# Moving QK products, softmax denominators, the exp table load and the output stores in a fused attention and MLP kernel

## The chip, the cores and the metric

The kernel runs as one program on 1 core of a Trainium2 chip. The metric is the device time of one launch in microseconds (us). The core has five engines that work from queues of their own: TensorE (PE: matmuls, with PEld for its weight loads), VectorE (DVE), ScalarE (ACT), GpSimd (POOL) and SyncE (SP, which only issues transfers here). An engine runs its instructions in the order in which they were written, and waits on semaphores where it needs another engine's result.

## The reference

One transformer block on 2048 tokens of width 576, bfloat16 in and out. Layer norm, a QKV projection, attention in which each token sees itself and 7 earlier tokens at distances of 2 (32 heads of 18), an output projection and a residual sum; then a second layer norm (applied twice in a row), an MLP of width 4608 with tanh GELU, and a second residual sum.

```python
idx = pos[:, None] - (jnp.arange(8) * 2)[None, :]
logits = jnp.einsum("bhsd,bhswd->bhsw", q, kg) * scale        # 8 keys of each token
attn = _softmax(jnp.where(mask, logits, -1e9))
o = jnp.einsum("bhsw,bhswd->bhsd", attn, vg)
h = x + o.reshape(B, S, D) @ wo
y = _layernorm(_layernorm(h))
out = h + _gelu(y @ w1 + b1) @ w2 + b2
```

## The kernel before, in words

**Tiles.** Token t lies in tile j = t mod 16, on partition t // 16, so there are 16 tiles of 128 tokens. With that layout the keys at distances of 2 lie in tiles of the same parity, in a ring of 8 (`k_ring`, `v_ring`). `halo` reloads one slot of a ring from a copy in DRAM, shifted by one partition, once the product that read the unshifted slot is done. The 16 tiles are taken in 8 pairs, `GROUPS[0]` to `GROUPS[7]`.

**Stages.** First all QKV products. Then a loop over k = 0 to 7, in which TensorE does the MLP of pair k, while VectorE and ScalarE do the attention of later pairs. The order of each engine is written out by hand (`tc.manual_schedule`): each piece of code that stands in a list is issued at that place. In the loop c, d are the tiles of pair k+1 and e, f those of pair k+2:

- `mlp1` is 4 visits of matmuls of the first MLP product, each followed by GELU on ScalarE. Each visit has 2 or 3 duos of banks. Between the first and the second half of a duo TensorE waits for a no-operation on GpSimd's queue (`marker`), which itself waits for the first half.
- `m1[0]` holds the output sums of the softmax, `pv_sum(c)` and `pv_sum(d)` (`att_pv_a`, line 399, is their first instruction), and the stores and transposing reads that bring the result back as `oT`. `m1[1]` holds the whole QK step of e: `att_qk_a` (line 344, one product of 128 x 4608) and `att_qk_b` (line 353, four halving adds, and line 360). `m1[3]` holds the first sums over GELU outputs (`h_sums`, line 650) that the second MLP product needs.
- `mlp2_fast` does the second MLP product (line 670) with 7 block products in place of 8, in an order given by `steps`. For k = 3 to 5 it is: "wo" (output projection of c and d into the banks pw), "hc" (`ln2_h(c)`, line 463, which reads pw on VectorE, and `ln2_act(c)`, lines 480 to 483), product 1, "b" (a copy of its bank on ScalarE, line 759), "h" (`ln2_h(d)`, `ln2_act(d)`, `put_b2`, more `h_sums`), product 7 into the bank that c's pw held, product 2 into the bank that "b" copied, product 6, "6" (`ln2_send(c)`: lines 489 and 175, and a store), "7" (`ln2_send(d)`; then QK of f; then `att_max`, lines 366 and 367), "d" (a copy, line 759), "rest" (a copy, line 727), "in" (the two transposing reads into `hnT`, line 499, the input of the next pair's `mlp1`; and `reload_x`), product 5, "f" (a copy), "exp" (line 385, and the GELU table again, line 539), product 4, "o1" (line 701: the second tile's output, and an accumulating transfer on GpSimd's queue, `out_sum`, line 772), "4" (`accumulate_h` on GpSimd's queue, line 511, behind the hnT reads; then `att_den`, lines 393 to 395), product 3, "o0".
- For k = 2 the order starts with product 1, and the product of f (line 344) already stands ahead of h, at the end of `m1[3]`.

**The statement that holds a product back.** `ln2_act` leaves the instruction of line 483 (a power on GpSimd, the reciprocal root of LN2) in `root`, and the next `att_qk_a` is made to wait for it:

```python
        if root[0] is not None:
            tc.add_manual_dep(ins, root[0].name, sync_dep, reason="products of QK behind the root of LN2")
```

**Stores.** The two output tiles of the pair before are stored by SP (`out_store`, line 775): tile j1 at "h" (ahead of `put_b2`, line 508), tile j0 at "6". SP also issues the stores of `hn` (lines 193, 194) and the hnT reads, in program order.

Of the kernel before, what the change touches and what calls it, by code (L numbers as in the profile page):

```python
# [8 lines left out]
ACT = mybir.ActivationFunctionType  # L9
ALU = mybir.AluOpType  # L10
# [7 lines left out]
def kernel(  # L18
# [12 lines left out]
    nc = tc.nc  # L31
    P = 128
    _, S, D = A_x.shape
# [3 lines left out]
    W = 8  # L37
# [34 lines left out]
    q_all = wpool.tile([P, NT, D], BF16, name="q_all")  # L72
# [265 lines left out]
            ring = (None, k_ring, v_ring)[t]  # L338
            nc.sync.dma_start(out=ring[j % 2][:, j // 2, :], in_=kv_dram[j, 0:P, t - 1, :])

    root = [None]

    def att_qk_a(j):
        ins = nc.vector.tensor_tensor(out=prod[:], in0=k_ring[j % 2], in1=q_all[:, j, :].unsqueeze(1)  # L344
                                      .to_broadcast([P, W, D]), op=ALU.mult).ins
        if root[0] is not None:
            tc.add_manual_dep(ins, root[0].name, sync_dep, reason="products of QK behind the root of LN2")
            root[0] = None

    def att_qk_add(j, steps):  # L350
        for o, a, c in steps:
# [124 lines left out]
    def ln2_act(j):  # L476
        h = h_of[j]
        y = sb.tile([P, D], BF16, tag="hn", name="hn", bufs=2)
        nmean, var, rstd = (sb.tile([P, 1], F32, tag=f"ln2_{t}", name=f"ln2_{t}", bufs=2) for t in ("nmean", "var", "rstd"))
        nc.scalar.activation(out=y[:], in_=h[:], func=ACT.Identity, scale=-1.0 / D, accum_out=nmean[:])  # L480
        nc.scalar.activation(out=y[:], in_=h[:], func=ACT.Square, bias=nmean[:], accum_out=var[:])
        nc.scalar.activation(out=var[:], in_=var[:], func=ACT.Identity, scale=(1.0 + EPS) / D, bias=eps2[:])  # L482
        ins = nc.gpsimd.tensor_tensor(out=rstd[:], in0=var[:], in1=mhalf[:], op=ALU.pow).ins  # L483
        root[0] = ins if j not in GROUPS[1] else None
        hn[j] = (h, rstd, nmean, y)

    def ln2_send(j):
# [50 lines left out]
    def gelu_table():  # L538
        nc.scalar.activation(out=warm[:], in_=mhalf[:], func=ACT.Gelu_apprx_tanh)


    NM = FT // 2
    fast = GROUPS[2:]
# [138 lines left out]
    def c_(fn, *a):  # L682
        return lambda: fn(*a)
# [4 lines left out]
    def mlp2_fast(g, rows, tags, wo, hooks, first_wo=False):  # L688
        last, summed = wo is None, rows < NM
        q, p, r, s = tags  # L690
        j0, j1 = g
        af = psum_pair(q, "po")
        a, f = (af[:, n, 0:HALF] for n in range(2))
        b, d = psum_pair(p, "po")[:, 0, 0:HALF], None
        o0, o1 = (new_o(j, summed) for j in g)
        flat = kv_ring[1][:].rearrange("p w t d -> p (w t d)")
        rest = halves(flat[:, W * 2 * D - 2 * D:W * 2 * D].bitcast(F32))
        bank = {1: a, 2: a, 3: f, 4: b, 6: b}

        def add(out, x, y):  # L700
            nc.vector.tensor_tensor(out=out, in0=x, in1=y, op=ALU.add)

        def last_out():
            nc.vector.tensor_copy(out=o0[:, HALF:HALF + HALF // 2], in_=f[:, 0:HALF // 2])
            nc.scalar.copy(out=o0[:, HALF + HALF // 2:D], in_=f[:, HALF // 2:HALF])
            nc.sync.dma_start(out=out3[:, j0, HALF:D], in_=o0[:, HALF:D])

        def out0(n0, n1):
            if summed:
                nc.scalar.copy(out=halves(o0), in_=af[:, :, 0:HALF])  # L710
                return
            add(halves(o0)[:, n0:n1], af[:, n0:n1, 0:HALF], halves(x_of(j0))[:, n0:n1])
            nc.sync.dma_start(out=out3[:, j0, n0 * HALF:n1 * HALF], in_=o0[:, n0 * HALF:n1 * HALF])

        def out1():
            if summed:
                add(o1[:, HALF:D], bank[5], o1[:, 0:HALF])
                add(o1[:, 0:HALF], b, o1[:, 0:HALF])
                out_sum(j1)
                return  # L720
            add(o1[:, 0:HALF], b, rest[:, 0])
            add(o1[:, HALF:D], bank[5], rest[:, 1])
            nc.sync.dma_start(out=out3[:, j1, :], in_=o1)

        def do_rest():
            if summed:
                nc.scalar.copy(out=o1[:, 0:HALF], in_=bank[7])
                return
            add(rest, bank[7].unsqueeze(1).to_broadcast([P, 2, HALF]), halves(x_of(j1)))

        def take():
            bank[7], bank[5] = (psum_pair(tag, "po")[:, 0, 0:HALF] for tag in (r, s))

        lo, hi, all_ = (0, SR), (SR, rows), (0, rows)
        seed = {"b": (1, 6), "d": (6, 5), "f": (5, 3)}
        does = {
            "wo": lambda: wo((r, s)), "e": take, "rest": do_rest, "o1": out1,
            "o0": lambda: last_out() if last else out0(0, 2), "lo": lambda: out0(0, 1),
            "11": lambda: plain(0, 0, a, rows), "12": lambda: plain(0, 1, f, rows),
            "21": lambda: plain(1, 0, b, rows), "22": lambda: plain(1, 1, bank[5], rows),  # L740
        }
        if rows < NM:
            steps = [(1, all_), "b", "wo", "hc", "h", "e", (2, all_), "11", (6, all_), "d", "6", "7", (7, all_), "rest"] if not first_wo \
                else ["wo", "hc", (1, all_), "b", "h", "e", (7, lo), (2, all_), (6, all_), "6", "d", "rest", "7", "11"] if rows == SR \
                else ["wo", "hc", (1, all_), "b", "h", "e", (7, lo), (2, all_), (6, all_), "6", "7", "d", "11", (7, hi), "rest"]
            steps += ["in", (5, all_), "f", "exp", (4, all_), "21", "22", "o1", "4", (3, all_), "12", "o0", "3"]
        elif not last:
            steps = ["wo", "hc", (1, all_), "b", "h", "e", (7, lo), (6, all_), "6", "d", "7", (2, all_), (7, hi), "rest", "in",
                     (5, all_), "f", (4, all_), "o1", "4", (3, all_), "o0"]
        else:  # L750
            steps = ["e", (1, lo), (7, lo), (1, hi), "b", "h", (7, hi), "rest", (6, all_), "d", (2, all_), "lo",
                     (5, all_), "f", (4, all_), "o1", (3, all_), "o0"]
        for step in steps:
            if isinstance(step, tuple):
                product(step[0], bank[step[0]], *step[1])
            elif step == "f" and last:
                add(f, bank[5], x_of(j0)[:, HALF:D])
            elif step in seed:
                nc.scalar.copy(out=bank[seed[step][1]], in_=bank[seed[step][0]])
            else:  # L760
                call([does[step]] if step in does else hooks.get(step, ()))
# [22 lines left out]
    with tc.manual_schedule(engines={ENG.PE, ENG.Activation, ENG.DVE, ENG.SP, ENG.Pool}):  # L784
# [227 lines left out]
        for k, g in enumerate(GROUPS):  # L1012
# [38 lines left out]
            if k < 6:  # L1051
                m1[1] = m1.get(1, []) + [c_(att_qk_one, e, 0)]
                m1.setdefault(3, [])
                if k == 2:
                    m1[0] += [c_(pv_sum, d), c_(send_o, d), c_(read_o, d)]
                    m1[3] += [c_(w2_sums, 0, 8, (2, 3)), c_(w2_sums, 8, 12, (2, 3)), c_(w2_sums, 12, 14, (0, 1)), c_(w2_sums, 14, 16, (0, 1)),
                              c_(att_qk_a, f), c_(halo, f, 1)]
                early = {2: (), 5: (0,)}.get(k, (0, 2))
                if k == 3:
                    m1[3] += [c_(w2_sums, 12, 14, (2, 3)), c_(w2_sums, 14, 16, (2, 3))]  # L1060
                m1[3] += [c_(h_sums, 0, min(rows, SR), early)]
                if k == 5:
                    x["h"] += [c_(h_sums, 0, SR, (2,)), c_(h_sums, 0, SR, (1, 3))]
                else:
                    x["h"] += [c_(h_sums, 0, SR, [t for t in range(4) if t not in early])]
                if rows > SR:
                    x["h"] += [c_(h_sums, SR, rows)]
                x["7"] += [c_(att_qk_one, f, 1) if k > 2 else c_(att_qk_b, f, 1), c_(att_max, (e, f))]
                x["exp"] += [c_(exps, e, f)]
                x["4"] += [c_(att_den, e, f)]  # L1070
            else:
                if k == 6:
                    ring1_free[0] = True
                    m1[1].append(c_(w2_sums, 16, NM))
                m1[3] = m1.get(3, []) + [c_(h_sums, 0, SR)]
                if k == 7:
                    mid[3] = {1: [c_(h_sums, SR, 16)]}
                    x["h"] += [c_(h_sums, 16, NM)]
# [16 lines left out]
                wo = lambda tags: wo_visit((c, tags[0]), (d, tags[1]))  # L1095
            if 3 <= k < 7:
                x["hc"].insert(0, c_(out_sum, GROUPS[k - 1][0]))
                x["h"].insert(0, c_(out_store, GROUPS[k - 1][1]))
                x["6"].insert(0, c_(out_store, GROUPS[k - 1][0]))
            mlp1(g, mlp1_plan(p, q, r, s, (r, s, p)), m1, mid)  # L1100
            if 3 <= k < 7:
                mlp2_fast(g, rows, (s, p, q, r), wo, x, True)
# [34 lines left out]
```

## Time and profile before

| | |
|---|---|
| median of 3 runs | 364.18 us (364.08 to 366.05) |
| the profiled execution: its time, its span | 363.63 us, 361.8 us |
| PE, DVE, ACT, POOL busy | 98%, 82%, 65%, 13% of the span |
| granted TensorE clock | 1.00 |
| start of the MLP of pairs 3, 4, 5, 6, 7 on PE | 180.85, 217.35, 253.14, 289.25, 324.92 us |
| VectorE's first output sum in pairs 3, 4, 5, 6 (line 399) | 181.30, 218.30, 254.41, 290.21 us |
| VectorE's first h in pairs 2, 3, 4, 5 (line 463) | 165.65, 201.35, 237.51, 273.08 us |

Lines of a timeline are: start, duration, engine, line, operation, output <- input, shapes, number of instructions, and in brackets the idle time before it with what ended it. Times are us from the span's start. A row of an engine ending in q is the queue that issues transfers.

### The profile page before, as it was taken

Reading aid. Unit: us, or ns where it says so; the run is one execution under the profiler, and the core shown is the slowest. Engines: PE = TensorE matmul, PEld = TensorE weight load, DVE = VectorE, ACT = ScalarE, POOL = GpSimd, SP = SyncE. Lnnn points to the kernel's source line nnn. Section 1 sums busy time; section 2 is a strip of 40 time slices with the busy share of each in tenths; the row PEclk is TensorE's granted clock in tenths of the full one; section 3 lists DMA queues with packets and bytes.
Section 4 is the critical chain, followed back from the end, with each engine's and each line's share of the span. In section 5 each row is a group of like instructions: output and inputs, shape, how many; then the busy total and the mean of one; then the engine's idle time right before and its main releaser. Section 6 shows DMA issues by size and latency. Waiting matters only on the chain.

```text
span 361.8 us, 11435 instructions
## 1 busy us (share of the span) xinstructions
PE 356.3 (98%) x4883; PEld 291.2 (80%) x4883; DVE 296.3 (82%) x417; ACT 235.5 (65%) x519; POOL 46.4 (13%) x61
## 2 busy tenths in 40 slices
PE   8999999999999999999999999999999999999996
PEld 5678777888778877887788778877887788779974
DVE  4999999999989999997799898989899998520431
ACT  4779846798646783668566955695669566706620
POOL 2241004000112020201110202020102110201000
PEclk9999999999999999999999999999999999999999
DMA  7986999973447884731454555445544252253001
GB/s 235 324 257 175 261 197 294 346 266 72 135 89 109 225 172 71 135 72 51 107 86 103 71 121 85 90 83 123 86 74 113 61 85 72 47 110 53 2 3 34
DMA packets 62980, 46.07 MB, mean 127 GB/s; under 512 B 32192, under 2 KB 60736, under 8 KB 62928
## 3 DMA queue, kind: packets, MB, share of 16 engines
q1 hardware_dynamic: 59024, 41.42, 44.2%
q0 software_dynamic: 3744, 3.84, 9.9%
q8 instruction: 38, 0.62, 0.7%
q10 hardware_dynamic: 160, 0.07, 0.1%
q14 instruction: 14, 0.11, 0.1%
HBM read 23.16 MB, written 12.42 MB: 98 GB/s over the span
## 4 chain that ended last, share of the span: by engine, by line
PE 91%; DMA 5%; ACT 1%; DVE 1%; issue 0%; ACTq 0%; SPq 0%
PE pm L217 37%; PE po L670 25%; PE pq L217 13%; PE po L582 10%; PE pw L217 5%; DMA oT<-td 2%; DMA xnT<-xd 1%; ACT h_all L563 1%; DMA wqh_sb<-in_A_wqkv_dram 1%; DMA x_all<-in_A_x_dram 1%; PE xt_pt L182 1%; DVE kv_ring L650 0%; DVE ln_stats L149 0%; PE h_pt L182 0%; PE o_pt L182 0%
## 5 line engine op out<-in xcount | busy, mean ns | idle before, releaser
L217 PE MATMUL pm<-hnT,w_sb 64*128 64x256 bf16 x2304 | 143.0, 269 | 0.1
L563 ACT ACTIVATE h_all<-pm,b_sb 128x256 f16<-128x256 f32 (+1 forms) x288 | 108.6, 496 | 51.2 <-PE pm L217 50.5
L217 PEld LDWEIGHTS <-w_sb 64*128 64x128 bf16 x2304 | 113.5, 94 | 13.4 <-issue 1.8
L670 PEld LDWEIGHTS <-h_all 128*128 128x128 f16 x480 | 46.2, 98 | 13.6 <-issue 1.6
L217 PE MATMUL pq<-wq_sb,xnT 64*128 64x288 bf16 x768 | 54.5, 283 | 0.3 <-DMA wq_sb<-in_A_wqkv_dram 0.2
L217 PEld LDWEIGHTS <-xnT 64*128 64x128 bf16 x864 | 41.8, 94 | 11.2 <-DMA xnT<-xd 0.4
L353 DVE TENSOR_TENSOR prod<-prod 128x2304 bf16<-128x2304 bf16 (+1 forms) x64 | 44.2, 691 | 2.0
L399 DVE TENSOR_TENSOR prod<-kv_ring,probs 128x4608 bf16<-128x4608 bf16 x16 | 40.9, 2558 | 2.6 <-DMA kv_ring<-kv_dram 2.2
L344 DVE TENSOR_TENSOR prod<-kv_ring,q_all 128x4608 bf16<-128x4608 bf16 x16 | 40.8, 2551 | 2.5 <-POOL ln_rstd L483 2.0
L217 PE MATMUL pm<-hnT,w1h_sb 64*128 64x256 bf16 x288 | 39.5, 269 | 0.0
L670 PE MATMUL po<-w2a_sb,h_all 128*128 128x288 bf16 (+1 forms) x262 | 35.8, 286 | 0.0
L405 DVE TENSOR_TENSOR prod<-prod 128x2304 bf16<-128x2304 bf16 (+1 forms) x32 | 33.9, 1058 | 1.1
L582 PEld LDWEIGHTS <-h_all 128*128 128x128 bf16 x288 | 27.9, 98 | 7.9 <-issue 1.0
L670 PEld LDWEIGHTS <-kv_ring 128*128 128x128 f16 x252 | 24.6, 98 | 6.3
L582 PE MATMUL po<-w2a_sb,h_all 128*128 128x288 bf16 x224 | 28.5, 286 | 0.0
L772 POOL DMA_DIRECT2D x_all<-o_sb x12 | 10.7, 889 | 126.9 <-PE pw L217 55.6
L650 DVE TENSOR_TENSOR kv_ring<-h_all 128x1536 f16<-128x1536 f16 (+3 forms) x9 | 6.8, 760 | 16.4 <-ACT h_all L563 16.4
L217 PE MATMUL pw<-wo_sb,oT 64*128 64x288 bf16 x256 | 19.6, 283 | 0.7 <-DMA oT<-td 0.7
L670 PE MATMUL po<-w2b_sb,h_all 128*128 128x288 bf16 (+1 forms) x122 | 19.7, 286 | 0.1
L162 POOL TENSOR_TENSOR ln_rstd<-ln_veps,mhalf 128x1 f32<-128x1 f32 (+2 forms) x14 | 13.4, 965 | 48.4 <-DVE ln_veps L156 33.3
L483 POOL TENSOR_TENSOR ln_rstd<-ln_var,mhalf 128x1 f32<-128x1 f32 x13 | 9.2, 708 | 80.9 <-ACT ln_var L482 80.9
L217 PEld LDWEIGHTS <-oT 64*128 64x128 bf16 x288 | 13.5, 94 | 5.3 <-DMA oT<-td 1.3
(115 smaller groups left out, 404.2 us busy)
## 6 DMA issues: line engine op xcount, KB each, us to landing
w_sb<-in_B_w_dram SPq DMA_DIRECT2D x6, 768.0 KB, 5.8
kv_ring<-kv_dram SPq DMA_DIRECT2D x28, 144.0 KB, 2.9
w2a_sb<-in_B_w_dram SPq DMA_DIRECT2D x4, 1008.0 KB, 7.1
kv_dram<-kv_ring SPq DMA_DIRECT2D x13, 288.0 KB, 3.3
td<-q_all SPq DMA_DIRECT2D x14, 144.0 KB, 1.8
x_all<-in_B_b_dram SPq DMA_DIRECT2D x14, 144.0 KB, 3.8
td<-hn SPq DMA_DIRECT2D x14, 144.0 KB, 1.8
x_all<-h POOLq DMA_DIRECT2D x14, 144.0 KB, 4.7
```

Source lines behind the costliest of these rows:

```text
L162: nc.gpsimd.tensor_tensor(out=rstd[:], in0=veps[:], in1=mhalf[:].to_broadcast([P, n]), op=ALU.pow)
L217: last = nc.tensor.matmul(duo["g"][r ^ swap][i], lhsT=lhsT, rhs=rhs, start=(swap == 0 and i == 0 and kt == 0), stop=(swap == 1 and kt == K ...
L344: ins = nc.vector.tensor_tensor(out=prod[:], in0=k_ring[j % 2], in1=q_all[:, j, :].unsqueeze(1) .to_broadcast([P, W, D]), op=ALU.mult).ins
L353: nc.vector.tensor_tensor(out=prod[:, :, o * H:o * H + n], in0=prod[:, :, a * H:a * H + n], in1=prod[:, :, c * H:c * H + n], op=ALU.add)
L399: nc.vector.tensor_tensor(out=prod[:].rearrange("p w (d h) -> p w d h", h=H), in0=v_ring[j % 2].rearrange("p w (d h) -> p w d h", h=H), in ...
L405: nc.vector.tensor_tensor(out=prod[:, 0:n, :], in0=prod[:, 0:n, :], in1=prod[:, n:2 * n, :], op=ALU.add)
L483: ins = nc.gpsimd.tensor_tensor(out=rstd[:], in0=var[:], in1=mhalf[:], op=ALU.pow).ins
L563: pace[0] = nc.scalar.activation(out=hT(grp)[:, f, 0:N], in_=ps[:, r, i * N:(i + 1) * N], func=ACT.Gelu_apprx_tanh, bias=b1_sb[:, f:f + 1] ...
L582: nc.tensor.matmul(banks[half], lhsT=hT(grp)[:, f, i * P:(i + 1) * P], rhs=w2_rows(f)[:, half * HALF:(half + 1) * HALF], start=(f == 0), s ...
L650: nc.vector.tensor_tensor(out=s_slot(t, m0, m1), in0=a, in1=b, op=alu)
L670: nc.tensor.matmul(bank, lhsT=l, rhs=r, start=start, stop=stop, skip_group_check=True)
L772: nc.gpsimd.dma_start(out=x_of(j), in_=o_of.pop(j), accum_op=ALU.add)
```

## The change

For pairs k = 3 to 5 the product of f (with the `halo` behind it) moves from "7" to the end of `m1[3]`, ahead of h, and its wait for the root of LN2 is gone. For k = 2, where the product already stood there, the first two of the four adds go with it. `att_den` moves from "4" to right behind `exps`, so that on VectorE its three instructions stand ahead of the two of line 701. The exp table, loaded until now by the exp itself behind the copy "f", is loaded by a one-column exp (`exp_table`) ahead of "in", that is, behind the copy "rest" and ahead of the copy "f"; the exp then needs no load. The two `out_store` of k = 3 to 6 stand together ahead of the sends at "6". On TensorE the order of instructions stays as it is; on GpSimd too.

```diff
     def att_qk_a(j):
-        ins = nc.vector.tensor_tensor(out=prod[:], in0=k_ring[j % 2], in1=q_all[:, j, :].unsqueeze(1)
-                                      .to_broadcast([P, W, D]), op=ALU.mult).ins
-        if root[0] is not None:
-            tc.add_manual_dep(ins, root[0].name, sync_dep, reason="products of QK behind the root of LN2")
-            root[0] = None
+        nc.vector.tensor_tensor(out=prod[:], in0=k_ring[j % 2], in1=q_all[:, j, :].unsqueeze(1)
+                                .to_broadcast([P, W, D]), op=ALU.mult)
...
+    def exp_table():
+        nc.scalar.activation(out=warm[:], in_=mhalf[:], func=ACT.Exp)
...
-            steps += ["in", (5, all_), "f", "exp", (4, all_), "21", "22", "o1", "4", (3, all_), "12", "o0", "3"]
+            steps += ["table", "in", (5, all_), "f", "exp", (4, all_), "21", "22", "o1", "4", (3, all_), "12", "o0", "3"]
...
-                              c_(att_qk_a, f), c_(halo, f, 1)]
+                              c_(att_qk_a, f), c_(halo, f, 1), c_(att_qk_add, f, ((0, 0, 9), (0, 0, 4)))]
...
                 m1[3] += [c_(h_sums, 0, min(rows, SR), early)]
+                if k > 2:
+                    m1[3] += [c_(att_qk_a, f), c_(halo, f, 1)]
...
-                x["7"] += [c_(att_qk_one, f, 1) if k > 2 else c_(att_qk_b, f, 1), c_(att_max, (e, f))]
-                x["exp"] += [c_(exps, e, f)]
-                x["4"] += [c_(att_den, e, f)]
+                x["7"] += [c_(att_qk_b, f, 1, 0 if k > 2 else 2), c_(att_max, (e, f))]
+                x["table"] = [exp_table]
+                x["exp"] += [c_(exps, e, f), c_(att_den, e, f)]
...
-                x["h"].insert(0, c_(out_store, GROUPS[k - 1][1]))
-                x["6"].insert(0, c_(out_store, GROUPS[k - 1][0]))
+                x["6"][0:0] = [c_(out_store, j) for j in GROUPS[k - 1][::-1]]
```

More of the change, by code (lines that the diff above doesn't have):

```diff
@@ L339, in halo @@
             nc.sync.dma_start(out=ring[j % 2][:, j // 2, :], in_=kv_dram[j, 0:P, t - 1, :])
-    root = [None]
     def att_qk_a(j):
-        ins = nc.vector.tensor_tensor(out=prod[:], in0=k_ring[j % 2], in1=q_all[:, j, :].unsqueeze(1)
-                                      .to_broadcast([P, W, D]), op=ALU.mult).ins
-        if root[0] is not None:
-            tc.add_manual_dep(ins, root[0].name, sync_dep, reason="products of QK behind the root of LN2")
-            root[0] = None
+        nc.vector.tensor_tensor(out=prod[:], in0=k_ring[j % 2], in1=q_all[:, j, :].unsqueeze(1)
+                                .to_broadcast([P, W, D]), op=ALU.mult)
     def att_qk_add(j, steps):
@@ L482, in ln2_act @@
         nc.scalar.activation(out=var[:], in_=var[:], func=ACT.Identity, scale=(1.0 + EPS) / D, bias=eps2[:])
-        ins = nc.gpsimd.tensor_tensor(out=rstd[:], in0=var[:], in1=mhalf[:], op=ALU.pow).ins
-        root[0] = ins if j not in GROUPS[1] else None
+        nc.gpsimd.tensor_tensor(out=rstd[:], in0=var[:], in1=mhalf[:], op=ALU.pow)
         hn[j] = (h, rstd, nmean, y)
```

## The prediction

> **What bounds the kernel now.** I read the page's busy shares and chain first.
>
> ```profile
> PE 356.3 (98%) x4883; PEld 291.2 (80%) x4883; DVE 296.3 (82%) x417; ACT 235.5 (65%) x519; POOL 46.4 (13%) x61
> PE 91%; DMA 5%; ACT 1%; DVE 1%; issue 0%; ACTq 0%; SPq 0%
> ```
>
> TensorE is busy for 98% and no matmul is removed, so the change can win no more than the waits of TensorE that it touches. The list of waits has them (the third row is a wait of VectorE):
>
> ```profile
> PE pw L217 <- DMA oT<-td: 0.7, 2, 0.6
> PEld L217 <- DMA oT<-td: 1.3, 2, 0.9
> DVE prod L344 <- POOL ln_rstd L483: 2.0, 2, 1.0
> ```
>
> Two waits for oT: in pair 3 the output projection took 3.03 us (198.54 to 201.57) where pair 4 took 2.30 (235.05 to 237.35), 0.73 lost; in pair 5 0.15. The most to be won is 0.9 us, 0.25%. A measurement of this kernel can tell about 0.5%, 1.8 us, from no change.
>
> So the question is what the moved work makes late. VectorE's timeline around h of pair 4:
>
> ```profile
> 236.63 0.96 DVE L650 TENSOR_TENSOR h_all<-h_all 128x1536 f16<-128x1536 f16 x1
> 237.51 1.42 DVE L463 TENSOR_TENSOR h<-pw,x_all 128x576 f32<-128x576 f32 x2
> 243.25 2.56 DVE L344 TENSOR_TENSOR prod<-kv_ring,q_all 128x4608 bf16<-128x4608 bf16 x1 [1.00 <-POOL ln_rstd L483]
> 250.56 0.69 DVE L367 TENSOR_TENSOR logits<-logits,peak 128x512 f32<-128x512 f32 x1
> 251.17 0.94 DVE L701 TENSOR_TENSOR o_sb<-po,o_sb 128x288 f32<-128x288 f32 x2
> 252.03 1.03 DVE L393 TENSOR_REDUCE den<-logits 128x64 f32<-128x512 f32 x1
> 254.41 2.56 DVE L399 TENSOR_TENSOR prod<-kv_ring,probs 128x4608 bf16<-128x4608 bf16 x1
> ```
>
> Before h there is no idle time: h is late because VectorE is. What hangs on h is in the ScalarE and TensorE timelines:
>
> ```profile
> 240.20 0.39 ACT L759 COPY po<-po 128x288 f32<-128x288 f32 x1
> 239.32 3.35 PE L670 MATMUL po<-w2a_sb,h_all 128*128 128x288 f16 x26
> ```
>
> The copy "b" ends 3.08 us after h begins, because ScalarE does c's statistics first. The 26 matmuls are 12 of product 7 and 14 of product 2; at 0.1225 us each product 2 begins at 240.79, and it writes the bank that "b" reads: only 0.2 us to spare.
>
> **The change, part by part.** All times below start at h, on the trace's clock.
>
> *Pair 2.* VectorE idles 2.47 us before h (163.18 to 165.65, for TensorE's pw). The two adds moved there cost 1.36 + 0.69, with gaps 2.1, and fit. Behind h 2.1 us go, so the maximum ends at 173.7 in place of 175.83. Then ScalarE is late: "rest" ends at 173.53, table and warm-up take 1.28 + 0.20, "f" 0.38, so the exp runs 175.45 to 176.1. Denominators 2.35 (252.03 to 254.38 in pair 4), line 701 0.95: output sums begin at 179.45 in place of 181.30.
>
> *Pair 3.* The sums feed oT, so oT comes 1.85 us earlier: TensorE's 0.73 is won. But on VectorE line 399 to h took 20.05 us (181.30 to 201.35) and now holds the product as well, 2.6: h at 202.1, 0.75 late. Product 2 would begin at 203.54 + 1.47 - 0.73 = 204.28; the copy it waits for ends at 202.1 + 3.08. With 0.06 for the semaphore that is 0.96 of stall. Net +0.23, and 0.15 from the next item.
>
> *The wait for the root that is taken away.* The product no longer idles 1.0 us, but the big add of line 353 (1.36 us) now runs when GpSimd wants to begin d's root, 5.16 us after h (242.67). GpSimd's timeline shows what that costs, with VectorE's of pair 1:
>
> ```profile
> 131.47 1.53 POOL L483 TENSOR_TENSOR ln_rstd<-ln_var,mhalf 128x1 f32<-128x1 f32 x1 [1.33 <-ACT ln_var L482]
> 240.45 0.75 POOL L483 TENSOR_TENSOR ln_rstd<-ln_var,mhalf 128x1 f32<-128x1 f32 x1 [2.47 <-ACT ln_var L482]
> 242.67 0.55 POOL L483 TENSOR_TENSOR ln_rstd<-ln_var,mhalf 128x1 f32<-128x1 f32 x1 [1.47 <-ACT ln_var L482]
> 131.24 1.35 DVE L640 TENSOR_TENSOR x_all<-w2a_sb 128x2304 f16<-128x2304 bf16 x1
> ```
>
> A root took 0.55 beside an idle VectorE; 131.47 + 1.53 = 133.00 is 0.41 after the end of the VectorE instruction that was running (132.59). The add will run 4.78 to 6.14 after h, so d's root ends at 6.56, not 5.71; d's send and the copy "d" come 0.5 later, 8.1 after h, where product 5 wants it at 8.0: 0.1 of stall, plus 0.05 for hnT, in pairs 3 and 4 (in pair 5 one more sum lies there). Bounds: 0 and 0.5 each. The Trainium skill's page "SBUF — State Buffer", section "Who interferes with whom", says that a VectorE instruction with two SBUF inputs and a GpSimd one that reads SBUF exclude each other, whichever starts first; it speaks against taking this wait away, and by it the root waits the add's remainder, 0.98 us; if it did not hold, 0.3 us of the whole sum would go.
>
> *Behind h.* Line 399 began 16.90 us after h. Minus the product 2.6, minus the root 1.0: 13.3. But the exp, which line 701 hid, lies open now: product 2 starts 3.14 after h; products 2, 6 and 5 take 1.96 each and two short blocks 0.98, so product 5 ends 10.1 after h with the 0.1 above; "f" takes 0.4, exp 0.65, denominators 2.35, line 701 0.95: 14.5. So VectorE's loop is 19.2 + 2.6 + 14.5 = 36.3 us against TensorE's 35.79: VectorE sets the pace, which the change does not shorten. The table is covered: "f" is needed by the blocks behind product 4, over 2 us later. Were it not, up to 1.3 us per pair. The Trainium skill's page "ScalarE: Activation LUTs", section "What ACT_TABLE_LOAD costs", adds a drain of 1.38 us to each load; no row shows it (after the load at 215.69 the warm-up begins 1.30 later), and by it the output sums would come 1.4 later and pairs 4 and 5 lose about 1.4 each, an estimate.
>
> *Pair 4.* Output sums at 202.1 + 14.5 = 216.6, h 21.8 later at 238.4. Product 2 is due at 240.79 + 0.38 = 241.17 and free at 241.54: +0.4, with the root +0.5. Shift now 0.9.
>
> *Pair 5.* Sums at 252.9. Line 399 to h took 18.67, less 0.32 idle, plus 2.6: h at 273.85. The product also needs the `halo` of e, issued 270.19 - 1.5 with 2.9 to land: 0.3 more, h at 274.15. Product 7 needs the sum that ended 2.29 after h: 276.5. It was due at 275.43 - 0.15 + 0.9 = 276.2. Shift 0.9 - 0.15 + 0.35 = 1.1; bounds of the halo 0 and 1.
>
> *Pair 6.* Only SP's order changes: one more `out_store` goes ahead of d's store.
>
> ```profile
> 316.05 0.43 SPq L193 DMA_DIRECT2D td<-hn  x1
> 320.53 2.53 SPq L499 DMA_TRANSPOSE hnT<-td  x2
> ```
>
> This store landed 4.3 us after issue, behind three transfers, where c's (313.75, nothing ahead) took 1.8: 0.8 for each transfer ahead. The second transpose (issued 321.8, 2.9 to land) arrives at 324.7 to 324.8; TensorE ended at 324.85 and began at 324.92. Nothing is spare, so 0.43 (one issue) to 0.8 reaches TensorE; I take 0.6. In pairs 3 to 5 I cost SP's new order at 0: the `halo` of f waits for the product, which ends as h begins, and `put_b2` behind it waits for h anyway; the second store waits for line 772's transfer (237.12 + 3.3 = 240.4), and the next thing behind it, c's store of hn, is ready only 6.1 after h, at 244.5. Each us by which that transfer lands past this would be paid in full.
>
> Sum: 0.4 + 0.5 + 0.2 + 0.6 = 1.7, rounded to 1.8 for the gaps left out. Span 363.6; the profiled execution took 1.83 more than its span: 365.4. It lay 0.55 below the median: **366.0 us**.
>
> **Rivals.**
>
> *A. Nothing is late.* If ScalarE's copies slip in, or VectorE's gaps shrink by the 0.5 us that its loop is over TensorE's, only the oT waits go: 0.9 less, 363.3. For it: the root's 1.0 is real. Against it: the copy had 0.2 to spare. It decides if pair 4's h begins before 238.0.
>
> *B. The accumulating transfers make GpSimd's queue late.* Line 701 now stands behind the denominators; behind it on GpSimd's queue come line 772 (begins 0.3 later), the two of line 511 (2.1 us in all), and then the marker on which TensorE waits 2.19 us into the next pair. Pair 4: line 701 ends at 252.9, so 252.9 + 0.3 + 0.6 + 2.1 = 255.9, and TensorE needs it at 253.14 + 0.9 + 2.19 = 256.2. Beyond 0.3 us of extra issue time each us is paid at pairs 3, 4 and 5: with 1 us, +2.1, 368.1. For it: line 511 will begin inside line 399's product. Against it: 1.75 us for both in pair 1 (147.39), beside line 405's adds.
>
> *C. The table costs nothing and does nothing.* The built order has one load for each, so a second load is not a rival of weight.
>
> **How the numbers follow.** Main case 0.56, 365.2 to 367.2, a little over half of it above the line of 0.5% (366.0): 0.31 slower, 0.25 same. B, or several narrow covers (GpSimd 0.3, hnT of pair 3 0.1) failing: 0.24, all slower. A 0.19: 0.15 same, 0.04 faster. Else 0.01 slower. Range 363.1 (A) to 368.6 (B and the upper bounds): 0.04 faster, 0.40 same, 0.56 slower.
>
> **What would show it.** Right: no oT wait of TensorE in pairs 3 and 5; first h at about 202.1, 238.4 and 274.2; a wait of TensorE for "b" or h ahead of product 2 or 7 of 0.3 to 1 us in each of these pairs; d's root longer than 1 us in pairs 3 and 4; VectorE idle about 0.7 us or more for the exp; pair 7's MLP behind a wait for hnT. Wrong: TensorE at 98% with MLP starts as before (A), or waits of TensorE's weight loads at the first marker of a pair (B).

## The result and the profile after

| | before | after |
|---|---|---|
| median of 19 runs each, same chip | 364.18 us (362.65 to 366.05) | 366.32 us (364.82 to 369.45) |
| ratio, 95% interval | | 1.0064 [1.0041, 1.0087] |
| the profiled execution: its time, its span | 363.63 us, 361.8 us | 367.51 us, 365.7 us |
| step of pairs 3, 4, 5, 6 | 36.50, 35.79, 36.11, 35.67 us | 37.82, 36.21, 36.49, 36.16 us |

A step is the time from the start of a pair's MLP on TensorE to that of the next pair. The change made the kernel 2.1 us slower, 0.6%. In the profiled executions the four steps cost 1.32, 0.42, 0.38 and 0.49, together 2.61. The other 1.28 us between the spans lies before the MLP of pair 0, which the change does not touch: TensorE waited 1.2 us for `q_all` there, 0.2 before. That start varied from 68.05 to 72.82 us over all kernels told of here, so kernels are compared below by their steps.

The page of the changed kernel, busy shares and chain:

```profile
PE 356.9 (98%) x4883; PEld 291.8 (80%) x4883; DVE 295.6 (81%) x417; ACT 236.0 (65%) x523; POOL 47.8 (13%) x61
PE 70%; DVE 13%; DMA 8%; ACT 5%; issue 2%; SPq 1%; POOL 0%; ACTq 0%; DVEq 0%; POOLq 0%
```

The busy row does not show the loss: 98% as before. The chain does: TensorE's share of it fell from 91% to 70% and VectorE's rose from 1% to 13%. The list of TensorE's waits (total, how often, longest) shows where:

```profile
PE po L667 <- DVE h L458: 1.0, 1, 1.0
PE pm L217 <- DMA hnT<-td: 0.9, 2, 0.6
PE po L667 <- ACT po L756: 0.7, 1, 0.7
PE po L667 <- DVE h_all L647: 0.5, 1, 0.5
```

The waits for oT are gone; h, the copy of its bank, the sums of `h_all` and hnT have taken their place. (The numbers of these lines are 2 to 6 lower in the changed kernel: 342 was 344, 458 was 463, 493 was 499.) TensorE's timeline in pair 3, where half of the loss is:

```profile
202.13 1.89 PE L667 MATMUL po<-w2a_sb,h_all 128*128 128x288 bf16 x14
203.85 0.41 PE L667 MATMUL po<-w2b_sb,h_all 128*128 128x288 bf16 x2
205.27 1.63 PE L667 MATMUL po<-w2a_sb,h_all 128*128 128x288 f16 x12 [1.01 <-DVE h L458]
207.60 1.88 PE L667 MATMUL po<-w2a_sb,h_all 128*128 128x288 bf16 x14 [0.70 <-ACT po L756]
```

The first two rows are product 1, the third product 7, the fourth product 2. Product 7 was due at 203.85 + 0.25 = 204.10 and began at 205.27, when h had read its bank; product 2 was due 1.47 later, at 206.74, and began at 207.60, behind the copy "b". 1.17 + 0.86 lost, less the 0.73 that oT cost before: 1.30 of the 1.32. VectorE's timeline of the same pair tells why h was late:

```profile
180.32 2.55 DVE L394 TENSOR_TENSOR prod<-kv_ring,probs 128x4608 bf16<-128x4608 bf16 x1
...
187.42 2.56 DVE L394 TENSOR_TENSOR prod<-kv_ring,probs 128x4608 bf16<-128x4608 bf16 x1 [1.88 <-DMA kv_ring<-kv_dram]
...
202.00 2.55 DVE L342 TENSOR_TENSOR prod<-kv_ring,q_all 128x4608 bf16<-128x4608 bf16 x1
204.47 1.41 DVE L458 TENSOR_TENSOR h<-pw,x_all 128x576 f32<-128x576 f32 x2
```

The output sums came early, as meant, but the second product of them waited 1.88 us for the reload of the v ring (0.18 before). In pair 4, the pair shown of before, VectorE ran like this:

```profile
237.80 2.55 DVE L342 TENSOR_TENSOR prod<-kv_ring,q_all 128x4608 bf16<-128x4608 bf16 x1
240.27 1.42 DVE L458 TENSOR_TENSOR h<-pw,x_all 128x576 f32<-128x576 f32 x2
...
251.42 1.06 DVE L388 TENSOR_REDUCE den<-logits 128x64 f32<-128x512 f32 x1 [1.10 <-ACT logits L380]
...
253.71 0.94 DVE L698 TENSOR_TENSOR o_sb<-po,o_sb 128x288 f32<-128x288 f32 x2
254.57 2.55 DVE L394 TENSOR_TENSOR prod<-kv_ring,probs 128x4608 bf16<-128x4608 bf16 x1
```

The product stands ahead of h; the sums begin 14.30 us after h where they began 16.90 after it; and VectorE now idles 1.10 us for the exp. d's root on GpSimd in pair 3, and SP's issues in pair 6:

```profile
209.63 1.26 POOL L478 TENSOR_TENSOR ln_rstd<-ln_var,mhalf 128x1 f32<-128x1 f32 x1 [1.47 <-ACT ln_var L477]
```

```profile
319.04 0.85 SPq L772 DMA_DIRECT2D out_dram<-x_all  x2
319.94 0.46 SPq L193 DMA_DIRECT2D td<-hn  x1
320.44 0.44 SPq L194 DMA_DIRECT2D td<-hn  x1
324.21 2.54 SPq L493 DMA_TRANSPOSE hnT<-td  x2
```

d's root took 1.26 in place of 0.55. In pair 6 the transposing read was issued 31.56 us after the pair's MLP began, before 31.28 (320.53 - 289.25).

### The profile page after: what moved, and what is told of

It is laid out like the page before. It is cut to its first block, busy times and chain, and to the rows that moved or that the text cites. A ratio compares the mean times of both kernels' runs of the same rounds, so it can differ in the third digit from the quotient of the medians.

```text
span 365.7 us, 11430 instructions
## 1 busy us (share of the span) xinstructions
PE 356.9 (98%) x4883; PEld 291.8 (80%) x4883; DVE 295.6 (81%) x417; ACT 236.0 (65%) x523; POOL 47.8 (13%) x61
## 4 chain that ended last, share of the span: by engine, by line
PE 70%; DVE 13%; DMA 8%; ACT 5%; issue 2%; SPq 1%; POOL 0%; ACTq 0%; DVEq 0%; POOLq 0%
PE pm L217 28%; PE po L667 15%; PE pq L217 13%; PE po L579 10%; PE pw L217 3%; DVE prod L394 3%; ACT h_all L560 2%; DVE prod L342 2%; DMA kv_ring<-kv_dram 2%; DVE prod L400 2%; DVE prod L348 2%; DMA x_all<-in_A_x_dram 1%; DMA xnT<-xd 1%; DMA wqh_sb<-in_A_wqkv_dram 1%; DMA td<-hn 1%
## 5 line engine op out<-in xcount | busy, mean ns | idle before, releaser
L478 POOL TENSOR_TENSOR ln_rstd<-ln_var,mhalf 128x1 f32<-128x1 f32 x13 | 10.6, 816 | 84.3 <-ACT ln_var L477 84.3
```

## The experiments

The theory to test: the product of f ahead of h costs about 5 us by itself, because VectorE's loop then grows past TensorE's 35.8; the denominators ahead of line 701 and the early table give most of that back; the missing wait for the root costs little because the product no longer stands next to it; the stores cost some tenths in pair 6. Rivals: the new place of the denominators costs (through GpSimd's queue), or the early output sums do (through the reload of the v ring). Rows with the same median of before ran on one chip and share its runs; the steps are those of one execution.

| kernel | median, before beside it | ratio, 95% | steps of pairs 3, 4, 5, 6 |
|---|---|---|---|
| x1_product | 369.65, 364.65 | 1.0154 [1.0130, 1.0178] | 38.34, 37.97, 38.36, 35.54 |
| x2_stores | 364.62, 364.65 | 1.0009 [0.9985, 1.0034] | 35.90, 36.28, 36.20, 36.05 |
| x3_product_back | 368.19, 364.65 | 1.0101 [1.0063, 1.0138] | 35.78, 37.97, 37.76, 36.84 |
| x5_no_root_wait | 366.49, 364.65 | 1.0052 [1.0031, 1.0073] | 37.10, 37.06, 35.79, 35.59 |
| x4_pair2 | 363.75, 363.86 | 0.9997 [0.9977, 1.0017] | 35.78, 35.78, 36.36, 35.71 |
| x6_stores_back | 366.91, 363.86 | 1.0069 [1.0047, 1.0091] | 38.07, 36.10, 35.79, 35.93 |
| x7_den_back | 370.59, 363.86 | 1.0167 [1.0136, 1.0199] | 38.31, 38.83, 36.73, 35.87 |
| x8_no_table | 370.19, 363.86 | 1.0172 [1.0128, 1.0217] | 37.92, 38.68, 37.18, 36.26 |
| x9_no_accumulate | 366.41, 363.48 | 1.0084 [1.0057, 1.0110] | 37.08, 35.88, 37.02, 36.80 |
| x10_again | 365.55, 363.48 | 1.0067 [1.0045, 1.0088] | 37.55, 35.88, 35.93, 35.91 |

**x1_product: the kernel before, with the product of f moved ahead of h alone** (and, as in the change, without its wait for the root).

```diff
+                if k > 2:
+                    m1[3] += [c_(att_qk_a, f), c_(halo, f, 1)]
...
-                x["7"] += [c_(att_qk_one, f, 1) if k > 2 else c_(att_qk_b, f, 1), c_(att_max, (e, f))]
+                x["7"] += [c_(att_qk_b, f, 1), c_(att_max, (e, f))]
```

> Before, with one part of the change alone: for pairs 3 to 5 the product of f stands ahead of h and waits for no root. The step of a pair is the start of the next pair's MLP on TensorE minus its own; before: 36.50, 35.79, 36.11, 35.67 us for pairs 3 to 6; changed kernel: 37.82, 36.21, 36.49, 36.16. Theory (h on VectorE is the limit, and the product ahead of it is what costs): worse than the whole change, since nothing else makes VectorE's loop shorter: first h of pair 3 at 203.9, products 7 and 2 wait some 2 us together there, and the loop 21.8 + about 16.2 = 38 us against 35.8, so steps of 38.5, 37.9 and about 38, +5 to +6 us in all. Rival (the product is free, the other parts cost): steps within 0.4 us of before, at most +1 us.

Measured: 5.0 us slower. VectorE's timeline of its pair 4 shows that the time the product freed behind h was not used:

```profile
241.36 1.41 DVE L460 TENSOR_TENSOR h<-pw,x_all 128x576 f32<-128x576 f32 x2
...
254.55 0.95 DVE L698 TENSOR_TENSOR o_sb<-po,o_sb 128x288 f32<-128x288 f32 x2 [3.14 <-PE po L667]
...
257.81 2.56 DVE L396 TENSOR_TENSOR prod<-kv_ring,probs 128x4608 bf16<-128x4608 bf16 x1
```

The output sums begin 16.45 us after h, hardly earlier than with the product behind it (16.90), because the o1 add waits 3.14 us for TensorE and the denominators stand behind it. The product is paid in full ahead of h and gives nothing back. The theory held.

**x7_den_back: the changed kernel with the denominators behind the o1 add.**

```diff
-                x["exp"] += [c_(exps, e, f), c_(att_den, e, f)]
+                x["exp"] += [c_(exps, e, f)]
+                x["4"] += [c_(att_den, e, f)]
```

> The changed kernel with the denominators put back behind the o1 add (line 698 of the changed kernel); exp and its early table stay. Theory (VectorE's loop sets the pace; the product ahead of h alone makes it 38.4, and the denominators ahead of the o1 add give back 2 of that): output sums begin 2 to 2.6 us later after h (16.5 to 16.9 in place of 14.3), steps of pairs 4 and 5 about 38 in place of 36.2 and 36.5, step of pair 3 unchanged or some tenths shorter (37.3 to 37.8), since the later output sums no longer meet the accumulating transfers; time 3 to 4 more, 369.5. Rival (the denominators wait for the exp anyway, 1.1 us, so their place is worth little): output sums 1 us later, steps 36.5 to 37, time 1 more.

```profile
217.39 0.95 DVE L698 TENSOR_TENSOR o_sb<-po,o_sb 128x288 f32<-128x288 f32 x2 [3.55 <-PE po L667]
218.25 1.03 DVE L388 TENSOR_REDUCE den<-logits 128x64 f32<-128x512 f32 x1
...
220.63 2.56 DVE L394 TENSOR_TENSOR prod<-kv_ring,probs 128x4608 bf16<-128x4608 bf16 x1
```

Measured: 6.7 us slower than before, 4 to 5 more than the changed kernel. The sums begin 16.79 us after the h at 203.84, and pair 4's step is 38.83. The wait of 3.55 for TensorE is the room that the denominators fill in the changed kernel: their move is a gain there, 2.5 us in pair 3 and 2.1 in pair 4 on VectorE. Pair 5's step was 36.73, not 38; pair 4 had given TensorE 3 us of delay already, which is the likely reason. Pair 3's step was not shorter (38.31). Its sums came late enough that VectorE did not wait for the v ring at all, and from the sums (181.49) to h (203.84) it took 22.35 us, the figure without that wait; but the sums began 2.3 us later than in x10_again (179.16), so oT was late again and cost 0.62. In pair 3 the loss thus has two forms of one size: late sums, or early sums that wait for the reload.

**x8_no_table: the changed kernel without the early table load.**

```diff
-                x["table"] = [exp_table]
```

> The changed kernel without its separate load of the exp table: the exp loads its table itself, behind the last bank copy. Theory (the table is on VectorE's path, because the denominators wait for the exp): exp 1.3 us later, VectorE's wait for it 2.2 to 2.4 in place of 1.1, output sums 15.6 us after h in place of 14.3, steps of pairs 4 and 5 37.0 to 37.5 in place of 36.2 and 36.5, time about 2 more, 368. Rival 1 (the exp has slack): steps and time as in the changed kernel. Rival 2 (a load costs a drain of 1.38 beside its 1.28, as the Trainium skill's page 'ScalarE: Activation LUTs', section 'What ACT_TABLE_LOAD costs', says): exp 2.7 later, steps 38 to 38.5; that sentence alone rests on the page.

```profile
220.73 1.04 DVE L388 TENSOR_REDUCE den<-logits 128x64 f32<-128x512 f32 x1 [2.55 <-ACT logits L380]
...
223.86 2.55 DVE L394 TENSOR_TENSOR prod<-kv_ring,probs 128x4608 bf16<-128x4608 bf16 x1
...
230.83 2.56 DVE L394 TENSOR_TENSOR prod<-kv_ring,probs 128x4608 bf16<-128x4608 bf16 x1 [1.68 <-DMA kv_ring<-kv_dram]
```

The wait for the exp grew in pair 3 from 1.15 and 1.18 (two executions of the changed kernel) to 2.55, and the sums begin 15.68 us after h (208.18), within 0.1 of the theory. The time is 6.3 us over before, 4 over the changed kernel, where 2 were expected. (The steps are those of its slowest execution, 374.46; 2.6 us of that are a wait of TensorE for xnT ahead of the pairs.) Pair 4's step rose by more than expected, to 38.68, because the later sums, with 1.68 for the v ring among them, made oT late too: TensorE waited 1.28 for it at 243.41. So the early load is worth its place: the table stood on VectorE's path. The growth of the wait, 1.37 to 1.40, is the 1.28 of the load and 0.1. The Trainium skill's page "ScalarE: Activation LUTs", section "What ACT_TABLE_LOAD costs", adds a drain of about 1.38 us to each switch; no run here shows one, since 2.66 would have made the wait 3.8, and the exp began 1.30 after its load (220.07 against 218.77).

**x5_no_root_wait: the kernel before with the wait for the root taken off, the product left behind h.**

```diff
-        if root[0] is not None:
-            tc.add_manual_dep(ins, root[0].name, sync_dep, reason="products of QK behind the root of LN2")
```

> Before, with nothing changed but that the product of f no longer waits for the root of LN2 (it stays behind h). Theory (VectorE's product and GpSimd's root keep each other off): the product begins 4.8 us after h, the root of d wants to begin at 5.16 and ends 0.42 after the product, at about 7.8 in place of 5.7: a root of 2.6 us in pairs 3 and 4, d's send and the copy d 2 us late, TensorE waits 1 to 1.6 us ahead of product 5 in those pairs, total +1 to +3 us. Rival (they share nothing): the root stays at 0.55 to 0.75 us, VectorE is 1.0 us earlier in pairs 3 and 4, and the time is the same or up to 0.3 us less.

GpSimd's, VectorE's and TensorE's timelines:

```profile
207.08 2.45 POOL L480 TENSOR_TENSOR ln_rstd<-ln_var,mhalf 128x1 f32<-128x1 f32 x1 [1.47 <-ACT ln_var L479]
```

```profile
206.57 2.55 DVE L344 TENSOR_TENSOR prod<-kv_ring,q_all 128x4608 bf16<-128x4608 bf16 x1
```

```profile
211.10 1.63 PE L667 MATMUL po<-x_all,kv_ring 128*128 128x288 f16 x12 [0.31 <-ACT po L756]
247.76 1.63 PE L667 MATMUL po<-x_all,kv_ring 128*128 128x288 f16 x12 [0.72 <-ACT po L756]
```

The product ended at 209.12, the root at 209.53, 0.41 later: a 2.45 us root in place of 0.55, and TensorE waits for the copy behind it, 0.31 and 0.72 where 1 to 1.6 were expected. The time rose by 1.8 us, so the wait that the change removes was worth its 1.0 us of idle VectorE while the product stood there. In the changed kernel only a 1.35 us add stands there, and the root's 1.26 made no product wait: from product 6 to product 5 TensorE took 2.94 us in pairs 3 and 4 (209.56 to 212.50, 245.36 to 248.30), as before (206.97 to 209.91).

**x3_product_back: the changed kernel with the product behind h again.**

```diff
-                if k > 2:
-                    m1[3] += [c_(att_qk_a, f), c_(halo, f, 1)]
...
-                x["7"] += [c_(att_qk_b, f, 1, 0 if k > 2 else 2), c_(att_max, (e, f))]
+                x["7"] += [c_(att_qk_one, f, 1) if k > 2 else c_(att_qk_b, f, 1, 2), c_(att_max, (e, f))]
```

(with the wait for the root)

> The changed kernel with the product of pairs 3 to 5 put back behind h and behind the root; all else as changed. Theory (product ahead of h is the cost): no wait of TensorE for h or for the copy b in pairs 3 to 5; the oT waits of pairs 3 and 5 stay away or shrink; steps about 35.9, 35.8, 35.9 and 36.2 for pair 6 (stores): 0.3 to 0.5 us below before, within noise of it, and 2 us or more below the changed kernel. Rival (denominators ahead of line 701, or the table, or the stores cost it): steps of pairs 3 to 5 stay above 36.2.

TensorE's rows, and the o1 add on VectorE:

```profile
219.88 2.36 PE L217 MATMUL pm<-hnT,w_sb 64*128 64x256 bf16 x40 [0.45 <-POOLq L227]
...
237.56 0.66 PE L217 MATMUL pw<-wo_sb,oT 64*128 64x288 bf16 x8 [1.39 <-DMA oT<-td]
217.67 0.94 DVE L704 TENSOR_TENSOR o_sb<-po,o_sb 128x288 f32<-128x288 f32 x2
```

The theory failed for pairs 4 to 6. Pair 3's step of 35.78 shows its wait for oT gone. But the first MLPs of pairs 4, 5 and 6 wait for the marker behind GpSimd's queue (0.45; the weight loads beside them 0.72), oT is 1.39 and 0.99 late in pairs 4 and 5, and VectorE waits 2.10 and 2.25 for the v ring. With the product behind h, the denominators do not fit ahead of the o1 add: it began 0.59 after the start of pair 4's MLP (217.08), where the changed kernel began it 2.05 ahead of that start (217.90 against 219.95). What hangs on that add is late: rival B of the prediction, which the changed kernel escapes. That the denominators do it, and not the table or the stores, is read from this place of the add; no run takes them apart. But the product ahead of h costs 5.0 us alone and the rest 3.5 without it, so the moves work only together.

**x4_pair2: the kernel before with pair 2's edits alone.**

```diff
-                              c_(att_qk_a, f), c_(halo, f, 1)]
+                              c_(att_qk_a, f), c_(halo, f, 1), c_(att_qk_add, f, ((0, 0, 9), (0, 0, 4)))]
...
-                x["7"] += [c_(att_qk_one, f, 1) if k > 2 else c_(att_qk_b, f, 1), c_(att_max, (e, f))]
+                x["7"] += [c_(att_qk_one, f, 1) if k > 2 else c_(att_qk_b, f, 1, 2), c_(att_max, (e, f))]
...
-                x["4"] += [c_(att_den, e, f)]
+                x["exp" if k == 2 else "4"] += [c_(att_den, e, f)]
```

> The kernel before, with the change in pair 2 alone: the two adds of the second tile (2.1 us) ahead of h, and the denominators ahead of the o1 add of line 701. The product of the second tile stays behind h in pairs 3 to 5, with its wait for the root; no second table load, stores as before. Theory (the product ahead of h is what costs; pair 2's own edits are free there): the output sums of pair 2 begin 1 to 2 us earlier than 181.30, TensorE's wait for oT in pair 3 (0.73) goes, and nothing else moves: step from pair 3 to pair 4 35.8 in place of 36.50, the others as before (35.8, 36.1, 35.7), time 0.7 less, 363.5. Rival 1 (the early output sums themselves cost, because the reload of the v ring then collides with the accumulating transfers of line 511, 1.9 us): h of pair 3 about 0.9 late, a wait for copy b or h of 0.7 in pair 3, step 36.4, no gain. Rival 2 (denominators ahead of line 701 delay the accumulating transfers on GpSimd's queue): a wait of TensorE for the marker at the start of pair 3, 0.7 to 1.2, which shows before pair 3's step.

VectorE's and TensorE's timelines:

```profile
186.02 2.56 DVE L399 TENSOR_TENSOR prod<-kv_ring,probs 128x4608 bf16<-128x4608 bf16 x1 [1.62 <-DMA kv_ring<-kv_dram]
...
200.66 1.41 DVE L463 TENSOR_TENSOR h<-pw,x_all 128x576 f32<-128x576 f32 x2
```

```profile
271.37 0.66 PE L217 MATMUL pw<-wo_sb,oT 64*128 64x288 bf16 x8 [0.40 <-DMA oT<-td]
```

Pair 3's step is 35.78, the 0.72 won as expected; pair 5 lost 0.25 of it to oT, which came 0.40 late. VectorE did wait for the reload, 1.62, but the sums began 2.12 earlier (179.18), so h still came 0.7 earlier than before. This is the only version whose steps are under those of before, by 0.44 in sum, and that is below what the times can show: 0.9997 [0.9977, 1.0017].

**x2_stores: the kernel before with the stores behind LN2's statistics.**

```diff
-                x["h"].insert(0, c_(out_store, GROUPS[k - 1][1]))
-                x["6"].insert(0, c_(out_store, GROUPS[k - 1][0]))
+                x["6"][0:0] = [c_(out_store, j) for j in GROUPS[k - 1][::-1]]
```

> Before, with the move of the output stores alone. Theory: nothing in pairs 3 to 5; step of pair 6 from 35.67 to 36.1 to 36.4, by a wait of TensorE for hnT at the start of pair 7, since one more transfer lies ahead of d's store of hn. Total +0.4 to +0.7 us. Rival (stores lie behind other transfers without cost): pair 6 stays at 35.7 and the step of pair 4, where the changed kernel waited 0.35 for hnT, shows that wait here too if the stores are its cause.

```profile
241.54 1.88 PE L670 MATMUL po<-w2a_sb,h_all 128*128 128x288 bf16 x14 [0.33 <-ACT po L759]
326.13 0.61 PE L217 MATMUL pm<-hnT,w_sb 64*128 64x256 bf16 x8 [0.45 <-DMA hnT<-td]
```

Pair 6's step rose by 0.38, with the wait for hnT as expected, and the transposing read was issued 31.70 us into the pair in place of 31.28. The time did not move measurably. Pairs 3 and 4 were expected to stay as they were and did not: pair 3's step fell by 0.60 in this execution, which has no wait for oT there, and pair 4's rose by 0.49, 0.33 of it a wait for the copy "b". Most of what the oT wait gave back was lost one pair later; whether the stores did either is not shown.

**x6_stores_back: the changed kernel with the stores at their old places** (the edit of x2 reversed).

> The changed kernel with SP's order of the output stores put back (one ahead of h, one at 6). Theory (behind LN2's statistics the stores stand in front of d's store of hn and its transposing read): step from pair 6 to pair 7 35.7 in place of 36.16, and the wait for hnT of 0.35 at pair 5's first MLP gone; together 0.5 to 0.9 less, 365.6. Steps of pairs 3 and 5 as in the changed kernel. Its pairs 2 and 3 are also those of the changed kernel up to h: if the reload of the v ring collides with the accumulating transfers by rule, VectorE's wait for it in pair 3's output sums is 1.5 to 2 us again and the step of pair 3 37.5 to 37.9; if the 1.88 us was an accident of one execution, 0.2 to 0.5 and 36.5 to 37.0. Rival (the store's place is free, the transposes are late because h is): steps and time as in the changed kernel.

```profile
255.16 0.61 PE L217 MATMUL pm<-hnT,w_sb 64*128 64x256 bf16 x8 [0.25 <-DMA hnT<-td]
326.88 0.61 PE L217 MATMUL pm<-hnT,w_sb 64*128 64x256 bf16 x8 [0.33 <-DMA hnT<-td]
```

Mostly a miss. The transposing read of pair 6 was issued earlier again (31.38), but TensorE still waited 0.33, and the step is still 0.26 over before. The wait at 255.16 was still there too, so that one is not the stores' doing. The time is that of the changed kernel. The stores account for 0.2 to 0.4 us of pair 6 by the issue of the read; more is not shown. Pair 3's step was 38.07, and VectorE's wait for the reload 2.12: no accident of one execution.

**x9_no_accumulate and x10_again: the reload of the v ring in pair 3.** x10_again is the changed kernel unaltered; x9_no_accumulate leaves out the two transfers of line 505 at the end of pair 2:

```diff
-                x["4"] = [c_(accumulate_hs, c, d)] + x["4"]
+                x["4"] = [c_(accumulate_hs, c, d) if k > 2 else lambda c=c, d=d: [h_of.pop(j) for j in (c, d)]] + x["4"]
```

> The changed kernel without the two accumulating transfers of line 505 that are issued at the end of pair 2 (so the rows of two tiles lack h); those of the other pairs stay. Theory (in pair 3 the reload of the v ring is late because these two transfers, issued in the same 2 us, hold the DMA engines): VectorE's wait for the reload ahead of the second product of output sums falls from 1.9 to 0.2 or less, h of pair 3 comes 1.7 us earlier, the two waits of TensorE at line 667 in pair 3 (1.01 and 0.70) go or keep 0.3 together, step from pair 3 to pair 4 36.1 to 36.9 in place of 37.82; steps of pairs 4 to 6 as in the changed kernel; time 1 to 1.7 less. Rival 1 (VectorE's own loop sets pair 3's step, not the reload): the wait shrinks, but line 394 to line 458 still takes 23 us or more and the step stays over 37.3. Rival 2 (the reload is late for another reason, the transfer of line 769 or its own queue): wait 1.5 to 2 again, step 37.8 to 38.1.

> The changed kernel, unaltered, as the control of the other kernel on the same chip and for what varies between executions. Theory: steps of pairs 3, 4 and 6 37.8, 36.2 and 36.1 again, with VectorE's wait for the reload in pair 3 1.5 to 2.1; pair 5's step between 35.8 and 36.5, since its wait for the halo (1.86 in the one execution, none with the stores put back) hangs on a transfer that lands within 1 us of its need. Rival (the 1.3 us of pair 3 was an accident of one execution): step of pair 3 36.7 to 37.1. Time 366.3 in both cases within 0.8.

VectorE's and TensorE's timelines, first of x10_again, then of x9_no_accumulate, and last the reload's row of x3_product_back:

```profile
186.01 2.56 DVE L394 TENSOR_TENSOR prod<-kv_ring,probs 128x4608 bf16<-128x4608 bf16 x1 [1.62 <-DMA kv_ring<-kv_dram]
```

```profile
203.86 1.63 PE L667 MATMUL po<-w2a_sb,h_all 128*128 128x288 f16 x12 [0.75 <-DVE h L458]
```

```profile
185.45 2.56 DVE L394 TENSOR_TENSOR prod<-kv_ring,probs 128x4608 bf16<-128x4608 bf16 x1 [1.15 <-DMA kv_ring<-kv_dram]
```

```profile
203.29 1.63 PE L667 MATMUL po<-w2a_sb,h_all 128*128 128x288 f16 x12 [0.27 <-DVE h L458]
```

```profile
185.51 2.56 DVE L399 TENSOR_TENSOR prod<-kv_ring,probs 128x4608 bf16<-128x4608 bf16 x1 [0.78 <-DMA kv_ring<-kv_dram]
```

The wait comes with the early sums. In seven executions the sums of pair 3 begin 1.8 us ahead of its MLP, and each waits for the reload: 1.88, 1.62, 2.12, 1.93, 1.62 and 0.78 (the changed kernel, x10_again, x6_stores_back, x8_no_table, x4_pair2, x3_product_back) with the two transfers, 1.15 without them. In the five in which they begin after its start (before, x1_product, x2_stores, x5_no_root_wait, x7_den_back) VectorE waited 0 to 0.18. What holds the reload is not shown. x9_no_accumulate lies inside the spread of the kernels that have the two transfers, and x3_product_back, which issues them at the same point of the pair, waited least, so their share cannot be read from one execution; the theory, that all but 0.2 is theirs, failed. Of the other transfers, line 769's (issued 179.46, 3.2 to land) was still under way when the reload was issued at 181.65; the two reloads of line 453 had landed by 181.5. And from 183.50 to 185.00, ahead of the end of its wait at 185.45, the DMA engines of x9_no_accumulate were busy for 4% and moved 6 GB/s, so the end of the reload did not stand behind a crowd of transfers there. Pair 3's step fell to 37.08; the copy "b" still cost 0.70 in both kernels. Pairs 5 and 6 of x9_no_accumulate lost more than pair 3 won (0.95 for the halo, 1.20 for hnT), and its time is that of the changed kernel. x10_again shows how far the other terms vary: pair 4's step 35.88 against 36.21, pair 5's 35.93 against 36.49, where VectorE waited 0.24 and 1.86 us for the same halo.

## Why the prediction was right

The time came out 0.3 us over the forecast of 366.0, and the mechanism is the forecast one: the oT waits go, h comes later than TensorE needs it, and the sum is a loss just past what can be measured. That the total came within 0.3 us is in part luck: pair 3 lost 0.7 to 0.9 more than forecast, and pairs 4 to 6 together as much as forecast in one execution (1.29 against 1.3) and 1.15 less in the other. By its terms:

| step | predicted | first execution | x10_again |
|---|---|---|---|
| pair 3 | +0.38 | +1.32 | +1.05 |
| pair 4 | +0.5 | +0.42 | +0.09 |
| pair 5 | +0.2 | +0.38 | -0.18 |
| pair 6 | +0.6 | +0.49 | +0.24 |
| sum | +1.7 | +2.61 | +1.20 |

- *The oT waits* went in pairs 3 and 5, and the table was covered, as worked out. Output sums were forecast 14.5 us after h; they came 14.3 after it in pairs 3 and 4.
- *Pair 3* is the term that was sized wrong, by 0.7 to 0.9. On the clock of before, the sums began at 179.04 (forecast 179.45) and h at 203.19 (forecast 202.1). The working took VectorE's 20.05 us from sums to h over unchanged and added the product: 22.65. Without a wait for the ring that is right (22.35 in x7_den_back), but starting the sums earlier also moved the reload of the ring, issued when their first product ends, to a time in which it landed late (4.4 us in place of 2.7), and 24.15 were needed. The prediction weighed what the moved instructions issue, and not what the earlier sums release.
- *Pair 4* was forecast as a wait for copy "b", of which none came. VectorE's loop is 35.8 us (204.47 to 240.27) and not 36.3: 21.5 + 14.3 against 21.8 + 14.5. With pair 3 having pushed TensorE back by 1.3, nothing was left to pay. What the first execution did lose, 0.35, was hnT, and x6_stores_back still had 0.25 of it with the stores back. The transposing read was issued 11.58 us after h, 9.22 before: 0.46 of that is d's store of hn, issued 7.67 after h in place of 7.21, the delay that the root was forecast to give, and nearly all the rest is the store's second part (line 194), which took 3.4 us to land in place of 1.6. Why it landed late stays open; it took 3.2 in x10_again, where TensorE did not wait.
- *The root* took 1.26 us where 1.40 was worked out (5.16 to 6.56 after h), but the 0.1 that product 5 was to pay behind it was not paid; 0 was the lower bound given. Its delay reached TensorE only through hnT, in pair 4. x5_no_root_wait shows at full size, 2.45 us, what the Trainium skill's page "SBUF — State Buffer", section "Who interferes with whom", says of such pairs, that they exclude each other; the row agrees with it.
- *Pair 5*: the halo's wait was put at 0.3 and was 1.86 in one execution and 0.24 in the other. The upper bound of 1 was too low; TensorE waited 0.53 for the sum of `h_all` in the first and not at all in the other, and the step stayed within 0.4 of the forecast either way.
- *Pair 6*: the wait for hnT came, and 0.6 was too high: steps of +0.24 and +0.49, and +0.38 with the stores alone in x2_stores. That the stores' order causes it is not shown for the changed kernel, since x6_stores_back, with the old order, still has +0.26.
- *Rival B* (GpSimd's queue late) did not show in the changed kernel and did in x3_product_back, which has the denominators' move without the product's. *Rival A* did not come: "b" and h held TensorE in pair 3, and pair 4's h began at 238.99 on the clock of before, past the 238.0 that was to decide.

## What to carry to other kernels

A busy engine that stands between two waits of the bounding engine has a loop of its own, and a move that shortens one half of it lengthens the other: add up the whole loop of that engine, per pair, before counting the wait that goes. Moves can be worth something only together: here the product ahead of h costs 5.0 us alone, the rest of the change without it 3.5, and all together 2.1. When work is started earlier, look also at what its end releases (here the reload of a ring): it starts earlier too, and may take longer there (3.3 to 4.7 us in place of 2.7).

## What the runs showed of the hardware

- A reload of 144 KB into the v ring, which lands in 2.7 us in pair 3 of the kernel before, took 4.4 in the first execution of the changed kernel, issued at 182.90 beside two accumulating transfers of 144 KB that GpSimd issued from 181.28 to 183.36. At the same point of the pair it took 3.3 to 4.7 in five other executions with these two transfers, and 3.7 in the one without them.
- A root on GpSimd that takes 0.55 us alone, and that became ready while a VectorE add or product ran, ended 0.41 to 0.42 us after that instruction, whether it was 1.35 us long (root 1.26, changed kernel) or 2.55 us long (root 2.45, x5_no_root_wait).
- Two executions of one kernel, with the same matmuls at the same clock, differed by 0.27, 0.33, 0.56 and 0.25 us in the steps of pairs 3 to 6, and with them differed the waits for transfers: 1.88 and 1.62 for the v ring in pair 3, 0.35 and none for hnT in pair 4, 1.86 and 0.24 for the halo in pair 5, 0.56 and 0.31 for hnT in pair 6. A term of this size that rests on one landing can be told from one trace only as a range.
